# Spreading the k/v sums of batches 4 to 7 over four steps each, in a fused linear-attention and mixture-of-adapters kernel

## The chip, the cores and the metric

The kernel runs on one core of a Trainium2 chip. The metric is the device time of one execution in microseconds (us), lower is better. The core has a matrix engine (TensorE, "PE" in the profile, with its weight loads as "PEld"), a vector engine (DVE), an activation engine (ACT), a general engine (POOL) and an engine that here only issues transfers (SP). Each works through its own list of instructions in order; they wait for each other through semaphores. Matrix products land in PSUM, which has eight banks of 512 float32 columns on 128 partitions, and DVE or ACT must copy ("evacuate") them from there into SBUF before a bank can be written anew.

## The reference, cut to what matters

```
# q, k, v: (8 batches, 8 heads, 576 positions, 64)
phi(x)  = concat(relu(x) * cos(theta_pos), relu(x) * sin(theta_pos))   # 64 -> 128 features
kv      = sum over positions of phi(k)^T v          # one 128 x 64 matrix per batch and head
z       = sum over positions of phi(k)
attn    = phi(q) kv / (phi(q) . z + 1e-6)
x       = attn as 4608 rows of 512
logits  = x @ w_gate                                 # 8 experts
w       = softmax over the two largest logits, 0 for the other six
out     = x + sum over e of  w[e] * (x @ A[e]) @ B[e]   # A[e]: 512 x 16, B[e]: 16 x 512
```

The sums `kv` and `z` of a batch run over all its positions, so they must be complete before the first row of that batch can be computed.

## The kernel before, in words

The 4608 rows are cut into 36 token tiles of 128 rows. A pair of batches has nine of them; the middle one (n = 4, 13, 22, 31) holds the last positions of both batches. Each batch is read in nine position slices of 64 rows, s = 0 to 8.

One trip of the loop `for n in range(NT - 1)` is called step n here. The order of the work is written out by hand: each engine gets its instructions in the order in which the loop emits them. In a step, PE does in this order:

- `move_q(n + 1)` (its matmuls at L213, from tile 27 on at L201): multiplies q of the next tile by diagonal matrices, which transposes it and scales it. The result fills two tiles of the pool `qd`, which has two banks; ACT evacuates both with a relu (`evac_q`, L229).
- `logits` (L300) of the tiles that `early_at` names, 4 matmuls for each tile: gate logits and the A products, into the bank `za`.
- `kv` (L180) of the position slices that `kv_at` names for this step, 8 matmuls for each slice. All slices of a batch are accumulated in the two banks `cd0` and `cd1`; after a batch's ninth slice `kv_out` (L188, ACT) copies the sums to SBUF.
- the outputs of this step: `emit` calls `delta` (L366: x times the identity, L371: the B product) and `evac_o` (L397, ACT copy), then stores through SP. From step 28 on (`add=n > 27`) it calls `delta_add` instead, which leaves out the L366 matmul and lets POOL add x (L391).
- `transp_x` (L274), the transposition of this tile's x, which waits for DVE's `normalise` (L259, L266), and in one step of three `transp_z` (L348).
- `logits` of the tiles that `late_at` names, and `numden(n + 1)` (L247, L252), numerator and denominator of the next tile, which needs both evacuated q tiles.

An output needs one bank. While no k/v sum is open it takes `cd0` and `cd1` in turn (`own`). In a step that has an entry in `kv_at` it takes one from the pool `qd`, q's banks, in the profile `dx`. The pool hands its two banks out in turn: a request waits until the tile that had the bank two requests before has been evacuated.

`todo` is the list of token tiles whose gates are ready; three tiles are added in one step of three. A step takes one of them, or two if more than three are waiting.

`kv_at` is filled by `put(kv_at, step, (b, s))`. With `first` the first step that uses batch b, a batch's first four slices are in step `first - 2` and the other five in step `first - 1`. For batches 4 to 7 these are the steps 16 and 17, 20 and 21, 25 and 26, 29 and 30. The scaled k that the sums read (`kp`) is made by POOL, two instructions a slice (L156), in order of s, begun in step 12, 17, 20 and 23 for these batches after a relu by DVE (L165); slice 8 of batches 4 and 5 is made by ACT (L151). k, q and v are loaded by transfers that POOL issues some batches ahead.

Of the kernel before, what the change touches and what calls it, by code (L numbers as in the profile page):

```python
# [19 lines left out]
def kernel(ctx, tc, q, k, v, w_gate, A, Bw, out):  # L20
# [43 lines left out]
    def load_k(b, eng=None):  # L64
        load(eng or nc.gpsimd, k_b[b].rearrange("p g s d -> p g (s d)"), k, b)

    def load_q(b):
        load(nc.gpsimd, q_b[b].rearrange("p g s d -> p g (s d)"), q, b)

    def load_v(b):  # L70
        load(nc.gpsimd, v_b[b][:, 0:VN].rearrange("p (g x) -> p g x", g=G), v, b)
# [36 lines left out]
    def make_diag(s):  # L108
        for i, tab in enumerate((cos_tab, sin_tab)):
            nc.vector.tensor_scalar(out=diag[:, s, i], in0=ident, scalar1=tab[:, s:s + 1],  # L110
                                    scalar2=None, op0=ALU.mult)
# [6 lines left out]
    def load_weights():  # L118
        nc.gpsimd.dma_start(out=AW[:, 0:E].rearrange("p e c r -> p e (c r)"),
                            in_=A.rearrange("e (p c) r -> p e (c r)", c=DCH))  # L120
        nc.gpsimd.dma_start(out=AW[:, E, :, 0:E],
                            in_=w_gate.rearrange("(p c) e -> p c e", c=DCH))
        nc.gpsimd.dma_start(out=Ball, in_=Bw.rearrange("e r d -> (e r) d"))
# [35 lines left out]
    def scale_k(b, s, eng=("pool", "pool")):  # L159
        for i, e in enumerate(eng):  # L160
            scale_k1(b, s, i, e)
# [13 lines left out]
    def kv(b, s):  # L175
        first, last = kv_n[b] == 0, kv_n[b] == NS - 1
        kv_n[b] += 1
        for g in range(G):
            for par, pr in enumerate((lo, hi)):
                nc.tensor.matmul(out=kvz[par][:, g], lhsT=kp_t[b][pr, s, g],  # L180
                                 rhs=v_rhs(b, g, s, pr),
                                 start=(first and g == 0), stop=(last and g == G - 1))

    def kv_out(b):
        kv_t[b] = t = p_kv.tile([128, 2, G, W], BF16, name="kvsb")
        for par in range(2):
            src = kvz[par].rearrange("p g u d -> p g (u d)")[:, :, 0:W]
            nc.scalar.copy(t[:, par], src)  # L188
# [189 lines left out]
    def delta_add(n, own=True):  # L378

        if own:  # L380
            dx = cd[dx_n[0] % 2]
            dx_n[0] += 1
        else:
            dx = qd.tile([128, DM], FP32, name="dx", tag="qd")
        g = group_of[n]
        nc.tensor.matmul(out=dx, lhsT=zgT_t[g][:, n - groups[g][0], :], rhs=Ball,
                         start=True, stop=True)
        osb_t[n] = dx
        evac_o(n)
        t = osb_t[n]  # L390
        nc.gpsimd.tensor_tensor(out=t, in0=t, in1=xt_t.pop(n), op=ALU.add)  # L391
# [21 lines left out]
    kv_at, relu_at, pool_at, act_at, dve_at = {}, {}, {}, {}, {}  # L413

    def put(at, step, what):
        at.setdefault(step, []).append(what)
# [6 lines left out]
    for b in range(2, B):  # L423
        first = b // 2 * NS + b % 2 * 4
        at = {2: 5, 3: 8, 4: 12, 5: 17, 6: 20, 7: 23}[b]
        n_pool = {2: 5, 3: 7, 4: 8, 5: 8}.get(b, 9)
        for s0, s1 in ((0, 3), (3, n_pool)):
            put(relu_at, at, (b, s0, s1))
        for s in range(n_pool):
            put(pool_at, at, (b, s))  # L430
        for i in range(2):
            if n_pool <= 7:
                put(dve_at, at, (b, 7, i))
            if n_pool < 9:
                put(act_at, first - 4 + i, (b, 8, i))
            if n_pool == 5:
                put(act_at, first - 3 + i, (b, 6, i))
                put(act_at, first - 2, (b, 5, i))
        order = (7, 0, 1, 2, 3, 4, 8, 6, 5) if n_pool <= 7 else (0, 1, 2, 3, 4, 5, 8, 6, 7)
        if n_pool == 9:  # L440
            order = range(NS)
        for j, s in enumerate(order):
            put(kv_at, first - (2 if j < 4 else 1), (b, s))

# [17 lines left out]
    with tc.manual_schedule():  # L464
        for s in range(6):
            make_diag(s)
        wu = qd.tile([128, DM], FP32, name="wu", tag="qd")
        for i in range(24):
            nc.tensor.matmul(out=wu, lhsT=ones, rhs=wide, start=True, stop=True)  # L469
        for s in range(NS):  # L470
            scale_k(0, s, ("act" if s < 7 else "dve", "dve"))
            kv(0, s)
        nc.scalar.activation(warm, halfpi, AF.Sigmoid)
        for s in range(6, NS):
            make_diag(s)
        load_k(1)
        load_v(1)
        load_q(1)
        load_k(2)
        load_weights()  # L480
        load_v(2)
        load_q(2)
        load_k(3)
        load_v(3)
        load_k(4)
        load_q(3)
        load_v(4)
        kv_out(0)
        transp_q(0)
        evac_q(0, 0, "dve")  # L490
        evac_q(0, 1)
        numden(0)

        g10, g11, g12 = range(len(groups) - 3, len(groups))
        todo, held = [], []
        first_loads = persist.tile([1, 8], BF16, name="first_loads")

        def emit(d, own=True, eng="act", add=False):
            if add:
                delta_add(d, own)  # L500
            else:
                delta(d, own)
                evac_o(d, eng)
            if held is None:
                store(d)
            else:
                held.append(d)

        for n in range(NT - 1):
            if n > 0:  # L510
                g = move_at.get(n - 1, (None,))[0]
                evac_x(n - 1, g)
                if g is not None:
                    todo += groups[g]
            normalise(n)
            if n != 3:
                move_q(n + 1)
            for t in early_at.get(n, ()):
                logits(t)
            for b, s in kv_at.get(n, ()):  # L520
                kv(b, s)
                if kv_n[b] == NS:
                    kv_out(b)
            if n == 3:
                move_q(n + 1)
            for g in gate_a_at.get(n, ()):
                gate_a(g)
            for g in gate_b_at.get(n, ()):
                gate_b(g)
            now = todo[:2 if len(todo) > 3 else 1]  # L530
            del todo[:len(now)]
            for d in now:
                emit(d, n not in kv_at, add=n > 27)
            for g in gate_a_at.get(n, ()):
                gate_sig(g)
            transp_x(n)
            for g in move_at.get(n, ()):
                transp_z(g)
            for b, s, i in dve_at.get(n, ()):
                scale_k1(b, s, i, "dve")  # L540
            for b, s0, s1 in relu_at.get(n, ()):
                relu_k(b, s0, s1)
            for b, s in pool_at.get(n, ()):
                scale_k(b, s)
                if (b, s) == pool_at[n][-1]:
                    if b + 3 < B:
                        load_k(b + 3)
                    if b + 2 < B:
                        load_q(b + 2)
                    if b + 3 < B:  # L550
                        load_v(b + 3)
                    if b + 3 == B - 1:

                        nc.sync.dma_start(out=first_loads, in_=k_b[B - 1][0:1, 0, 0, 0:8])
                        for d in held:
                            store(d)
                        held = None
            for t in late_at.get(n, ()):
                logits(t)
            numden(n + 1)  # L560
            for b, s, i in act_at.get(n, ()):
                scale_k1(b, s, i, "act")


        evac_x(NT - 2)
        normalise(NT - 1)
        transp_z(g10)
        logits(NT - 2)
        evac_z(g10, [("act", 0, 3)])
        todo += groups[g10]  # L570
        for d in todo[:-3]:
            emit(d)
        transp_x(NT - 1)
        gate_a(g11)
        emit(todo[-3])
        gate_sig(g11)
        evac_x(NT - 1)
        logits(NT - 1)
        gate_b(g11)
        emit(todo[-2])  # L580
        gate_a(g12)
        transp_z(g11)
        evac_z(g11, [("act", 0, 2)])
        gate_sig(g12)
        emit(todo[-1])
        gate_b(g12)
        emit(NT - 3)
        transp_z(g12)
        evac_z(g12, [("dve", 0, 1)])
        emit(NT - 2)  # L590
        emit(NT - 1, eng="dve")
# [28 lines left out]
```

## Time and profile before

| | us |
|---|---|
| median of 3 runs | 116.12 (116.11 to 116.18) |
| the profiled execution, its own time | 116.03 |
| its span, first to last instruction | 114.3 |
| PE busy | 99.1 (87% of the span) |
| DVE busy | 79.8 (70%) |
| ACT busy | 77.6 (68%) |
| POOL busy | 71.2 (62%) |
| steps 14 to 30, from the first L213 of step 14 to the first L201 of step 31 | 45.77 (49.03 to 94.80) |

The profile is of one execution. Its page has the busy time of each engine, the span in 40 slices, the chain of work that ended last, and groups of instructions by line. A row of the timeline gives the start in us, the duration, the engine and line, the operands, the count of instructions merged into the row, and in brackets the idle time of the engine before it with what ended it. Matmuls overlap, and the ends of their records are modelled, so what a block of matmuls costs is read from its start to the start of the next block.

### The profile page before, as it was taken

The numbers are of one execution on the slowest core, as the hardware profiler recorded it, in microseconds if no ns is written. First come the engines' busy times: TensorE is split into PE (matmuls) and PEld (weight loads), VectorE is DVE, ScalarE is ACT, GpSimd is POOL, SyncE is SP. The second block draws the span as 40 slices with busy tenths as digits, with TensorE's granted clock in tenths as the row PEclk, the third lists the DMA queues.
The fourth block names the chain that finished last, engine by engine and source line by source line (L and its number), as shares of the span: only waits on it lengthen the run. The fifth ranks groups of instructions, "written<-read, shape, count | busy, mean of one in ns | idle before, by whom it ended". The sixth has DMA issues, their size and how long they took to land.

```text
span 114.3 us, 5021 instructions
## 1 busy us (share of the span) xinstructions
PE 99.1 (87%) x2101; PEld 73.9 (65%) x2101; DVE 79.8 (70%) x280; ACT 77.6 (68%) x169; POOL 71.2 (62%) x133
## 2 busy tenths in 40 slices
PE   3999677877998999999999999999998998978710
PEld 1347466756895688768787687787866886755200
DVE  5697588569849859697657966899459378796620
ACT  5087679846995847588758956777568668785720
POOL 5992222248986994999359989989940444744000
PEclk9999999999999999999999999999999999999996
DMA  3999999999999999999999999999989331433792
GB/s 43 384 207 209 212 202 207 205 187 210 207 212 205 207 209 209 209 207 208 207 209 207 207 208 231 279 336 379 356 324 383 126 100 71 154 127 141 269 331 88
DMA packets 19670, 24.77 MB, mean 217 GB/s; under 512 B 2624, under 2 KB 14528, under 8 KB 19648
## 3 DMA queue, kind: packets, MB, share of 16 engines
q0 software_dynamic: 13856, 13.84, 72.8%
q1 hardware_dynamic: 5792, 10.62, 26.4%
q8 instruction: 16, 0.26, 0.9%
q14 instruction: 6, 0.05, 0.1%
HBM read 28.85 MB, written 9.44 MB: 335 GB/s over the span
## 4 chain that ended last, share of the span: by engine, by line
PE 49%; DMA 26%; DVE 13%; issue 4%; POOL 3%; ACT 2%; POOLq 0%; ACTq 0%
DMA k<-in_k_dram 14%; DMA v<-in_v_dram 12%; PE cd L180 10%; PE za L300 8%; PE qd L213 6%; PE nd L252 6%; PE xz L274 5%; DVE xt L266 4%; PE qd L201 3%; PE dx L366 2%; DVE xT L280 2%; DVE zg L335 2%; PE cd L366 2%; PE cd L371 2%; PE xz L348 2%
## 5 line engine op out<-in xcount | busy, mean ns | idle before, releaser
L229 ACT ACTIVATE qpT<-qd 128x512 bf16<-128x512 f32 x71 | 38.6, 595 | 15.9 <-PE qd L213 11.7
L280 DVE COPY xT<-xz 128x512 bf16<-128x512 bf16 (+1 forms) x36 | 17.1, 475 | 15.2 <-PE xz L348 8.4
L156 POOL TENSOR_SCALAR kp<-k,cos_tab 128x256 bf16<-128x256 bf16 x46 | 22.5, 490 | 7.3 <-DVE k L165 6.4
L266 DVE TENSOR_TENSOR xt<-nd,rden 128x512 bf16<-128x512 f32 x36 | 24.9, 691 | 1.2
L156 POOL TENSOR_SCALAR kp<-k,sin_tab 128x256 bf16<-128x256 bf16 x46 | 21.8, 475 | 0.0
L180 PE MATMUL cd<-v,kp 64*128 64x128 bf16 x576 | 18.7, 217 | 0.7 <-DMA v<-in_v_dram 0.7
L274 PEld LDWEIGHTS <-xt 128*128 128x128 bf16 x144 | 10.4, 116 | 13.5 <-DVE xt L266 10.6
L252 PE MATMUL nd<-kvsb,qpT 128*128 128x65 bf16 (+1 forms) x320 | 17.2, 195 | 1.3 <-ACT qpT L229 0.5
L274 PE MATMUL xz<-ident,xt 128*128 128x128 bf16 x144 | 14.5, 223 | 4.3 <-DVE xt L266 4.2
L180 PEld LDWEIGHTS <-kp 64*128 64x128 bf16 x576 | 16.2, 94 | 2.5 <-issue 0.7
L213 PE MATMUL qd<-diag,q 128*64 128x128 bf16 x432 | 17.2, 222 | 0.1
L391 POOL TENSOR_TENSOR osb<-osb,xt 128x512 f32<-128x512 f32 x7 | 8.1, 1158 | 11.8 <-ACT osb L397 11.8
L397 ACT COPY osb<-cd 128x512 f32<-128x512 f32 x24 | 13.9, 594 | 1.3 <-PE cd L371 1.2
L252 PEld LDWEIGHTS <-qpT 128*128 128x128 bf16 (+1 forms) x320 | 12.5, 99 | 2.2 <-ACT qpT L229 1.2
L213 PEld LDWEIGHTS <-q 128*64 128x64 bf16 x432 | 12.9, 109 | 1.5 <-DMA q<-in_q_dram 0.3
L300 PE MATMUL za<-AW,xT 128*128 128x144 bf16 x140 | 12.2, 227 | 0.7 <-DVE zg L335 0.7
L247 PE MATMUL nd<-eps_hi,ones 128*128 128x4 bf16 x72 | 11.6, 169 | 0.0
L300 PEld LDWEIGHTS <-xT 128*128 128x128 bf16 x144 | 9.1, 98 | 2.9 <-DVE xT L280 0.8
L259 DVE RECIPROCAL rden<-nd 128x8 f32<-128x8 f32 x36 | 7.2, 201 | 5.2 <-PE nd L252 5.1
L62 POOL DMA_DIRECT2D v<-in_v_dram x8 | 6.2, 780 | 5.2 <-DMA q<-in_q_dram 4.3
L469 PE MATMUL wu<-wide,ones 128*128 128x512 bf16 x24 | 7.5, 488 | 2.0 <-DVE AW L115 2.0
L397 ACT COPY osb<-dx 128x512 f32<-128x512 f32 x11 | 6.4, 594 | 3.8 <-PE dx L371 3.0
(73 smaller groups left out, 137.7 us busy)
## 6 DMA issues: line engine op xcount, KB each, us to landing
out_dram<-osb SPq DMA_DIRECT2D x32, 256.0 KB, 3.7
v<-in_v_dram POOLq DMA_DIRECT2D x8, 576.0 KB, 17.9
q<-in_q_dram POOLq DMA_DIRECT2D x8, 576.0 KB, 16.2
k<-in_k_dram POOLq DMA_DIRECT2D x7, 576.0 KB, 15.5
k0f<-in_k_dram SPq DMA_DIRECT2D x1, 1152.0 KB, 5.4
out_dram<-osb SPq DMA_DIRECT2D x8, 128.0 KB, 3.8
AW<-in_moe_A_dram POOLq DMA_DIRECT2D x1, 128.0 KB, 18.2
Ball<-in_moe_B_dram POOLq DMA_DIRECT2D x1, 128.0 KB, 16.6
```

Of the source, the lines that this page charges most:

```text
L156: nc.gpsimd.tensor_scalar(out=dst, in0=src, scalar1=tab, scalar2=1.0, op0=ALU.mult, op1=ALU.mult)
L180: nc.tensor.matmul(out=kvz[par][:, g], lhsT=kp_t[b][pr, s, g], rhs=v_rhs(b, g, s, pr), start=(first and g == 0), stop=(last and g == G - 1))
L213: nc.tensor.matmul(out=t[cols, j, 2 * gi:2 * gi + 2, :], lhsT=q_b[b][:, 2 * gp + gi, s, :], rhs=diag[:, s, i], start=(j == 0 and gi == 0), ...
L229: nc.scalar.activation(t, src, AF.Relu)
L247: nc.tensor.matmul(out=nd[:, gg, D:4 * W:W], lhsT=ones, rhs=eps_hi, start=True, stop=False, skip_group_check=True)
L252: nc.tensor.matmul(out=nd[pr, gg, j * W:(j + 1) * W], lhsT=qpT[:, j, pr], rhs=kv_t[b][:, h % 2, h // 2, :], start=False, stop=(j == 3), sk ...
L266: nc.vector.tensor_tensor(out=x, in0=nd[:, :, :, 0:D], in1=rden.rearrange("p (g j) -> p g j", g=2).to_broadcast([128, 2, 4, D]), op=ALU.mult)
L274: nc.tensor.transpose(out=xz[:, c * 128:(c + 1) * 128], in_=x[:, c], identity=ident)
L280: nc.vector.tensor_copy(t[:, 0:c], xz[:, 0:c * 128].rearrange("p (c s) -> p c s", c=c))
L300: nc.tensor.matmul(out=za_t[g][:, i, :], lhsT=xT[:, c, :], rhs=AW[:, :, c, :], start=(c == 0 and i == 0), stop=(c == DCH - 1), skip_group_ ...
L391: nc.gpsimd.tensor_tensor(out=t, in0=t, in1=xt_t.pop(n), op=ALU.add)
L397: nc.scalar.copy(t, src)
```

## The change

For batches 4 to 7 the nine slices are spread over four steps: two slices each in the steps `first - 4`, `first - 3` and `first - 2`, three in `first - 1`. The second edit limits a step that has an entry in `kv_at` to one output. Batches 0 to 3 and the functions that are called stay as they are.

```
         for j, s in enumerate(order):
-            put(kv_at, first - (2 if j < 4 else 1), (b, s))
+
+            ahead = (2 if j < 4 else 1) if b < 4 else 4 - min(j // 2, 3)
+            put(kv_at, first - ahead, (b, s))
...
-            now = todo[:2 if len(todo) > 3 else 1]
+            now = todo[:2 if len(todo) > 3 and n not in kv_at else 1]
             del todo[:len(now)]
             for d in now:
                 emit(d, n not in kv_at, add=n > 27)
```

The steps with sums of batches 4 to 7 become 14 to 21 and 23 to 30, which are all steps from 14 to 30 but 22. In these the outputs go through `qd`.

## The prediction, written before the changed kernel had run

> **What bounds the kernel now.** I read the page first: busy times and the chain that ended last.
>
> ```profile
> PE 99.1 (87%) x2101; PEld 73.9 (65%) x2101; DVE 79.8 (70%) x280; ACT 77.6 (68%) x169; POOL 71.2 (62%) x133
> PE 49%; DMA 26%; DVE 13%; issue 4%; POOL 3%; ACT 2%; POOLq 0%; ACTq 0%
> ```
>
> PE is the busiest engine and has half of the chain; the loads' quarter of it is the start of the span, before the steps that change. So the next view was PE's timeline over two steps that hold the sums of batch 4 now, 16 and 17, read from start to start.
>
> ```profile
> 53.96 0.64 PE L213 MATMUL qd<-diag,q 128*64 128x128 bf16 x16
> 54.53 1.07 PE L180 MATMUL cd<-v,kp 64*128 64x128 bf16 x32
> 55.53 0.39 PE L366 MATMUL dx<-xt,ident 128*128 128x512 bf16 x1
> ...
> 56.41 0.39 PE L274 MATMUL xz<-ident,xt 128*128 128x128 bf16 x4
> 56.63 0.17 PE L247 MATMUL nd<-eps_hi,ones 128*128 128x4 bf16 x1
> ...
> 57.02 0.69 PE L213 MATMUL qd<-diag,q 128*64 128x128 bf16 x16
> 57.65 0.67 PE L300 MATMUL za<-AW,xT 128*128 128x144 bf16 x8
> 58.25 1.29 PE L180 MATMUL cd<-v,kp 64*128 64x128 bf16 x40
> 59.47 0.39 PE L366 MATMUL dx<-xt,ident 128*128 128x512 bf16 x1
> ```
>
> Nothing waits here: one block follows the other. It gives the price list. The transposition of q is 0.57 (53.96 to 54.53). A block of 32 sum matmuls is 1.00, one of 40 is 1.22: 0.0275 for a matmul and a fixed 0.12 for a block. Two outputs are 0.88 (55.53 to 56.41), so one is 0.44 and its B product alone about 0.22. x is 0.22, numerator and denominator 0.39. Last, the steps where PE does wait. Each row of the view of stretches is a step: start and end, its length, then busy time and number of instructions of PE, PEld, DVE, ACT and POOL, the granted clock, DMA share and GB/s. They are the steps 14, 16, 19, 22, 24, 27, 28, 31 and 33.
>
> ```profile
> 49.03:51.92 2.89, 2.71 (x45) 1.99 (x42) 2.23 (x6) 2.52 (x7) 2.89 (x7) 1.00 1.21 207
> 53.96:57.02 3.06, 3.06 (x70) 2.35 (x68) 2.08 (x6) 2.45 (x7) 1.29 (x2) 1.00 1.21 207
> 63.00:65.03 2.03, 1.92 (x35) 1.23 (x32) 1.96 (x6) 2.03 (x6) 2.03 (x6) 1.00 1.22 209
> 71.86:73.72 1.86, 1.82 (x42) 1.18 (x38) 1.60 (x6) 1.44 (x4) 1.86 (x5) 1.00 1.14 277
> 76.01:78.12 2.11, 2.11 (x39) 1.42 (x37) 2.04 (x11) 1.60 (x5) 2.11 (x5) 1.00 1.08 373
> 84.40:86.37 1.97, 1.97 (x55) 1.35 (x52) 1.90 (x10) 1.39 (x4) 0.00 (x0) 1.00 0.90 338
> 86.37:88.58 2.21, 1.64 (x51) 1.12 (x49) 2.04 (x6) 1.66 (x5) 0.00 (x0) 1.00 1.04 378
> 94.80:96.84 2.04, 1.70 (x53) 1.18 (x49) 1.86 (x5) 1.56 (x5) 1.17 (x1) 1.00 0.03 8
> 98.76:100.72 1.96, 1.73 (x55) 1.23 (x52) 1.89 (x10) 1.60 (x4) 1.16 (x1) 1.00 0.39 142
> ```
>
> A step without sums whose contents by the price list are q 0.57, one output 0.44, x 0.22 and nd 0.39 should take 1.62. Step 19 takes 2.03, so PE waits 0.41 in it; step 22 waits 0.24; step 24, with 4 logit matmuls at 0.26 more, 0.23. In these ACT and DVE are busy 1.4 to 2.0: they set the short steps, PE the long ones. That is where the change can win: it moves PE work from the long steps into the short ones.
>
> **The change part by part.** (a) More blocks. Eight steps get a block of 16 sum matmuls: 14, 15, 18, 19, 23, 24, 27, 28. The number of matmuls stays, so a batch goes from 2 to 4 fixed parts: 8 x 0.12 = 0.96. Where logits come right before the sums there is more:
>
> ```profile
> 74.29 0.67 PE L300 MATMUL za<-AW,xT 128*128 128x144 bf16 x8
> ...
> 74.80 0.38 PE L366 MATMUL cd<-xt,ident 128*128 128x512 bf16 x1
> ```
>
> Eight logit matmuls take 0.51 ahead of an output but 0.60 ahead of sums (57.65 to 58.25). Sums run in another tile shape (64\*128) than logits and outputs (128\*128), so I take 0.10 for each change of shape after logits. That meets five of the new steps (15, 18, 23, 24, 27): 0.50. Together +1.46 of PE. No block of 16 is in this trace; the ends are 0.44 (16 x 0.0275, no fixed part) and 0.66 (both changes paid), and I take 0.56, or 0.66 after logits, by the line through 32 and 40, which are the nearest rows. The ends move the sum by -1.46 and +0.30.
>
> The Trainium skill, "TensorEngine Tiling (Array Packing)", Key Properties, states that changing the tiling mode, not just the tile, drains TensorE; it speaks against spreading the sums, and the 0.10 and 0.12 above agree with it. The drain of about 128 cycles that the skill's "TensorE: Matmul & The Clock Gate" (Step-by-step) gives would be an estimated 0.053 at 2.4 GHz, and with two for each of eight blocks 0.85 in place of 1.46, so a time 0.6 lower; the rows decide.
>
> (b) Outputs. Following `todo` through both rules: steps 14 to 30 emit 20 outputs now (5 to 24) and 18 after (5 to 22). The double steps 14, 16 and 18 become single, 22 becomes double, and the missing two are caught up as second outputs of 31 and 33. Three of the outputs are cheap `delta_add` ones, now (tiles 22 to 24) as after (20 to 22). So two full outputs leave the stretch: -0.88. In 31 and 33 they are B products alone, 0.22 each, and those steps have contents of about 1.2 and 1.5 in 2.04 and 1.96: the waits cover them (without that cover +0.44). ACT copies and POOL adds one more tile in each of the two, where ACT is busy 1.6 of 2.0 and POOL 1.2: a small delay is possible, none is counted. From step 33 on the list of outputs is that of now, so the tail, the stores on SP's queue included, stays.
>
> (c) Waits of PE that the added 0.56 covers. 19: 0.41. 24: 0.23. 22: 0.24, by its second output. 27: contents 1.69 (q's transposition is 0.38 here, by the next fence) in 1.97; of the 0.28 about 0.11 is the wait of (d), so 0.17. 14:
>
> ```profile
> 51.04 0.66 PE L300 MATMUL za<-AW,xT 128*128 128x144 bf16 x8 [0.18 <-DVE zg L335]
> ...
> 86.37 0.45 PE L201 MATMUL qd<-diag,q 64*64 64x64 bf16 x32
> 86.75 0.39 PE L386 MATMUL cd<-Ball,xT 128*128 128x512 bf16 x1
> 87.53 0.41 PE L274 MATMUL xz<-ident,xt 128*128 128x128 bf16 x4 [0.39 <-DVE xt L266]
> ...
> 88.34 0.30 PE L252 MATMUL nd<-kvsb,qpT 128*128 128x65 bf16 x4 [0.18 <-ACT qpT L229]
> ```
>
> In 14 the logits start 2.01 after the step because DVE's gate must end first. Sums 0.56 and one output instead of two put PE there at 1.79, so 0.2 of 0.34 stays: 0.14 won. Step 28 has contents of 1.21 (0.38 + 0.22 + 0.22 + 0.39) in 2.21: 1.00 of waits. Of these 0.38 stays by (d), 0.62 is won. Sum (c): -1.81.
>
> (d) New waits, the price of q's banks. In each step with sums the output takes a `qd` bank, so it waits for ACT's first evacuation of q, and everything on PE behind it (x, nd, the next q) waits too; and the next transposition of q waits for ACT's copy of the output.
>
> Rows of ACT's timeline, then of PE's:
>
> ```profile
> 54.48 1.08 ACT L229 ACTIVATE qpT<-qd 128x512 bf16<-128x512 f32 x2
> 80.33 0.59 ACT L397 COPY osb<-dx 128x512 f32<-128x512 f32 x1 [0.61 <-PE dx L371]
> 87.20 1.09 ACT L229 ACTIVATE qpT<-qd 128x512 bf16<-128x512 f32 x2 [0.55 <-PE cd L386]
> 80.74 0.67 PE L201 MATMUL qd<-diag,q 64*64 64x64 bf16 x32
> 81.34 0.67 PE L300 MATMUL za<-AW,xT 128*128 128x144 bf16 x8
> ```
>
> In step 16 ACT starts 0.52 after PE's transposition; one evacuation is about 0.6, and PE follows ACT after 0.05 (87.20 + 1.09, then 88.34). So the bank is free at 1.17. With 32 sums PE comes at 1.57, with 16 at 1.13: a wait of 0.04, in 16, 19 and 25; with logits ahead of the sums PE comes at 1.4 or later. From step 26 on the transposition fills both banks at once, so it waits for the output's copy at its very start: step 26 after the dx of 25 takes 0.60 (80.74 to 81.34; the copy ends at 80.92) against 0.38 undisturbed. That 0.22 comes newly in 28 and 29. In 28 ACT can start only when both tiles are done, so the output waits about 0.18 as well; these are the 0.38 of (c). New on top: 3 x 0.04 + 0.2 = +0.3. Ends: 0 for each of the 12 steps with 16 sums, and 0.31, the lateness of ACT in step 28 now (87.20 is 0.83 after 86.37, against 0.52), so 0 to +3.7; I stand near the low end because the rows of step 16, which is of the same kind, give 0.04.
>
> (e) Earlier need of data.
>
> ```profile
> 60.00 0.47 POOL L156 TENSOR_SCALAR kp<-k,sin_tab 128x256 bf16<-128x256 bf16 x1
> 26.01 0.76 POOL L62 DMA_DIRECT2D v<-in_v_dram  x1
> DMA to landing us min/median/max: 7.6/17.9/21.1
> ```
>
> POOL's list is not changed. Batch 5 is the closest: its slices 0 and 1 are scaled by 60.5 (the sine of slice 1 is the row of 60.00), counted from a relu early in step 17, which starts at 57.02. Slice 0 is needed 0.57 + 0.36 into step 18, thus 61.6 on the old clock and about 61.1 with the shortened steps 16 and 17; slice 1 a quarter of a microsecond later. It holds by some tenths. v of batch 4 is issued at 26.01 and lands by 47.1 even at the slowest landing; it is needed at 49.6. Cost 0; should POOL be late, up to 0.5 once.
>
> Sum: 1.46 - 0.88 - 1.81 + 0.32 = -0.9. On the profiled execution's own 116.03 (span 114.3) that is 115.1; the median of the runs, 116.12, is 0.09 above it, so 115.2.
>
> **Rivals.** First, q's banks bind (slower). Place: L366 in the 12 steps with 16 sums, behind ACT's first evacuation. (a) to (c) give -1.23; the wait decides from 0.10 in each of the 12 steps on. At 0.2 it is +2.4 - 1.2 = +1.2: 117.3. For it: the margin in step 16 is nil, ACT is late by 0.3 in step 28 now, and after the change each late copy delays the next transposition, which delays ACT. Against it: steps 17, 21 and 26 follow outputs in q's banks now and wait 0 to 0.22 (17: 0.06, 57.02 to 57.65), and a step has only about 1.7 of regular ACT work.
>
> The Trainium skill has the same fear in "TensorEngine Tiling (Array Packing)", PSUM Bottleneck: a faster TensorE leaves the PSUM copies as the bottleneck.
>
> Second, no change: the short steps are set by the loop nd, DVE, x, nd rather than by PE, and work put into them does not shorten the long ones as much as counted. If a third of (c) is won, 0.6 instead of 1.81, the sum is +0.3 and with fewer switches about 0: 116.1. For it: DVE is busy 2.04 of 2.11 in step 24 and 1.90 of 1.97 in step 27. Against: in the long steps PE has no wait, and they get shorter by 0.4 to 0.9 each.
>
> Third, scaled k comes late (slower): POOL holds up steps 18 to 21 and then everything behind; 0.5 for each of batches 5 and 6 makes 116.2 or more. The margins of (e) speak against it. That the outputs don't go through `qd` cannot be: `n not in kv_at` decides it.
>
> **How the numbers follow.** Forecast and near it (114.6 to 115.8) 0.58; the banks 0.25; no change 0.12; late k 0.05. A difference of 0.2% (0.23 us) is about what can be told from none. So faster 0.58, same 0.12, slower 0.30. The range goes from 114.6 (no new wait and 0.2 less for the blocks) to 117.0, with the outer part of the banks' case, about 0.15, above it and 0.05 below; the forecast's own range is 114.6 to 115.8.
>
> **What the profile after should show.** L180 in blocks of 16 and 24 that take 0.56 and 0.78; steps 16, 17, 20, 21, 25, 26, 29 and 30 shorter by 0.3 to 0.9, 15, 23, 24 and 27 longer by 0.4 to 0.7; little idle PE ahead of L366; the first L201 of step 31 near 94.0. I am wrong if L366 waits for ACT by more than 0.1 in most steps, if L201 waits by more than 0.3, or if steps 18 to 21 wait for POOL.

## The result, and the profile after

The changed kernel takes 115.44 us (115.39 to 115.54, 4 runs) against 116.12 (116.06 to 116.18, 4 runs) on the same chip: a ratio of 0.9939, 95% interval 0.9921 to 0.9956. It is faster by 0.6%. The profiled execution took 115.39 with a span of 113.6; before, 116.03 and 114.3. From the page of the changed kernel, the busy times and the chain by engine:

```profile
PE 99.4 (88%) x2099; PEld 74.2 (65%) x2099; DVE 80.9 (71%) x280; ACT 78.1 (69%) x169; POOL 73.2 (64%) x135
PE 52%; DMA 26%; DVE 11%; POOL 3%; issue 2%; ACT 2%; POOLq 0%; DVEq 0%; ACTq 0%
```

PE is still the bound, and its share of the chain is larger. Next, the view of stretches for the same nine steps as in the prediction (14, 16, 19, 22, 24, 27, 28, 31, 33), then the whole of steps 14 to 30, with the same columns:

```profile
49.06:51.95 2.89, 2.86 (x59) 2.27 (x56) 2.31 (x6) 2.23 (x6) 2.89 (x7) 1.00 1.21 208
54.65:56.86 2.21, 2.21 (x53) 1.73 (x50) 2.08 (x6) 2.02 (x6) 0.60 (x1) 1.00 1.21 207
62.56:64.83 2.27, 2.23 (x51) 1.78 (x48) 1.88 (x6) 2.08 (x6) 2.27 (x7) 1.00 1.21 208
70.76:72.79 2.03, 2.03 (x42) 1.43 (x38) 1.75 (x6) 1.61 (x5) 2.03 (x5) 1.00 1.18 237
75.74:78.39 2.65, 2.61 (x56) 1.95 (x54) 2.22 (x11) 1.52 (x4) 2.65 (x6) 1.00 1.06 390
83.80:86.26 2.46, 2.46 (x71) 1.87 (x69) 2.03 (x10) 1.52 (x4) 0.09 (x1) 1.00 0.84 313
86.26:88.49 2.23, 2.04 (x66) 1.65 (x64) 1.88 (x6) 1.75 (x5) 0.00 (x0) 1.00 0.72 265
94.02:96.06 2.04, 1.91 (x54) 1.20 (x48) 1.86 (x5) 1.56 (x5) 1.16 (x1) 1.00 0.22 79
98.02:99.97 1.95, 1.95 (x57) 1.32 (x54) 1.88 (x10) 1.57 (x4) 1.71 (x2) 1.00 0.41 154
...
49.06:94.02 44.96, 44.65 (x1020) 35.06 (x1017) 34.01 (x106) 33.02 (x72) 33.26 (x67) 1.00 1.00 239
```

Step 16 went from 3.06 to 2.21. Steps 24 and 27 grew, from 2.11 to 2.65 and from 1.97 to 2.46, because they hold sums now. Steps 14, 31 and 33 kept their length with more PE work in them. The stretch shrank from 45.77 to 44.96, by 0.81, and the rest of the execution gave 0.17 of that back. PE's timeline shows steps 16 and 17, and then 28, of the changed kernel:

```profile
54.65 0.64 PE L213 MATMUL qd<-diag,q 128*64 128x128 bf16 x16
55.22 0.62 PE L180 MATMUL cd<-v,kp 64*128 64x128 bf16 x16
55.82 0.38 PE L366 MATMUL dx<-xt,ident 128*128 128x512 bf16 x1
...
57.43 0.67 PE L300 MATMUL za<-AW,xT 128*128 128x144 bf16 x8
58.04 0.84 PE L180 MATMUL cd<-v,kp 64*128 64x128 bf16 x24
58.81 0.39 PE L366 MATMUL dx<-xt,ident 128*128 128x512 bf16 x1
...
86.84 0.62 PE L180 MATMUL cd<-v,kp 64*128 64x128 bf16 x16
87.65 0.38 PE L386 MATMUL dx<-Ball,xT 128*128 128x512 bf16 x1 [0.19 <-ACT qpT L229]
```

A block of 16 sums is 0.60 in step 16 with the small wait of the output in it, a block of 24 is 0.77, and only in step 28 does the profile mark the output as waiting for ACT's evacuation of q.

### The profile page after: what moved, and what is told of

It reads as the page before. It is cut to its first block, busy times and chain, and to the rows that moved or that the text cites. A ratio compares the mean times of both kernels' runs of the same rounds, so it can differ in the third digit from the quotient of the medians.

```text
span 113.6 us, 5022 instructions
## 1 busy us (share of the span) xinstructions
PE 99.4 (88%) x2099; PEld 74.2 (65%) x2099; DVE 80.9 (71%) x280; ACT 78.1 (69%) x169; POOL 73.2 (64%) x135
## 4 chain that ended last, share of the span: by engine, by line
PE 52%; DMA 26%; DVE 11%; POOL 3%; issue 2%; ACT 2%; POOLq 0%; DVEq 0%; ACTq 0%
DMA k<-in_k_dram 14%; DMA v<-in_v_dram 12%; PE cd L180 10%; PE za L300 8%; PE qd L213 7%; PE nd L252 6%; PE xz L274 5%; PE dx L366 4%; DVE xt L266 4%; PE qd L201 3%; PE dx L371 3%; PE xz L348 2%; DVE zg L335 2%; DVE xT L280 2%; ACT qpT L229 1%
## 5 line engine op out<-in xcount | busy, mean ns | idle before, releaser
L180 PE MATMUL cd<-v,kp 64*128 64x128 bf16 x576 | 20.1, 217 | 0.8 <-DMA v<-in_v_dram 0.8
L180 PEld LDWEIGHTS <-kp 64*128 64x128 bf16 x576 | 16.2, 94 | 3.4 <-issue 0.8
L252 PE MATMUL nd<-kvsb,qpT 128*128 128x65 bf16 (+1 forms) x320 | 16.9, 194 | 1.0 <-DVE qpT L231 0.5
L391 POOL TENSOR_TENSOR osb<-osb,xt 128x512 f32<-128x512 f32 x9 | 10.2, 1160 | 9.5 <-ACT osb L397 9.0
L397 ACT COPY osb<-dx 128x512 f32<-128x512 f32 x18 | 10.6, 591 | 5.3 <-PE dx L371 5.0
L252 PEld LDWEIGHTS <-qpT 128*128 128x128 bf16 (+1 forms) x320 | 12.4, 99 | 1.7 <-ACT qpT L229 0.7
L247 PE MATMUL nd<-eps_hi,ones 128*128 128x4 bf16 x72 | 11.6, 169 | 0.0
L397 ACT COPY osb<-cd 128x512 f32<-128x512 f32 x17 | 9.7, 599 | 1.3 <-PE cd L371 1.3
```

The costliest lines, as they stand in the source:

```text
L247: nc.tensor.matmul(out=nd[:, gg, D:4 * W:W], lhsT=ones, rhs=eps_hi, start=True, stop=False, skip_group_check=True)
L252: nc.tensor.matmul(out=nd[pr, gg, j * W:(j + 1) * W], lhsT=qpT[:, j, pr], rhs=kv_t[b][:, h % 2, h // 2, :], start=False, stop=(j == 3), sk ...
L397: nc.scalar.copy(t, src)
```

## The experiments

All ratios are to the kernel before, run beside it on the same chip. Lengths of steps 14 to 30 come from PE's timeline, from the first transposition of q of step 14 to that of step 31. Four kernels were profiled twice; for three of them the two lengths agree within 0.01, the fourth is told of at the end. A whole execution can shift by some tenths in the first 45 us (step 14 starts between 48.90 and 49.71 in the profiles of kernels that are alike up to there), so these lengths are the sharper measure.

**Each edit alone.** First the spreading without the limit (the changed kernel with one line undone), then the limit without the spreading (that line alone in the kernel before):

```
-            now = todo[:2 if len(todo) > 3 and n not in kv_at else 1]
+            now = todo[:2 if len(todo) > 3 else 1]
```

> Only the first edit: the sums of batches 4 to 7 over four steps, while a step may still emit two outputs. Theory A (the gain is PE work put into waits, minus shape changes, and the two outputs that leave steps 14 to 30 are needed for it): 1.46 for the blocks, nothing for outputs, waits covered in 14, 19, 24, 27 and 28 of about 1.8, new waits 0.3, so 0.0 against before: 116.1. Theory B (spreading the sums is the gain, the limit to one output does nothing): 115.4, as the changed kernel.

> Only the second edit: sums in two steps as before, but one output at most in a step with sums. The second output of step 16 (0.44 of PE, no wait there) moves to step 24, where 0.23 of it falls into a wait. Theory A: 0.2 faster than before, 115.9. Theory B: no change, 116.1. If the limit alone makes the gain: 115.4.

Spreading alone took 116.57, ratio 1.0035 (1.0018 to 1.0051): slower. The limit alone took 115.86, ratio 0.9969 (0.9956 to 0.9982), a stretch of 45.56, the 0.2 less of theory A (0.36 by the medians, on a chip where the kernel before scattered from 115.84 to 116.68). It holds back only the second output of step 16, because in the kernel before only eight of these steps have sums. Theory B falls, and so does the thought that the limit alone makes the gain. Rows of the view of stretches for the run that only spreads: steps 14 to 30, and step 28.

```profile
49.71:95.94 46.23, 44.92 (x1012) 35.41 (x1021) 33.26 (x106) 34.00 (x74) 33.26 (x67) 1.00 1.00 241
87.90:90.41 2.51, 2.04 (x67) 1.66 (x64) 1.88 (x6) 1.75 (x5) 0.00 (x0) 1.00 0.74 272
```

The stretch is 0.46 longer than before where theory A had 0.0. Step 28 explains 0.28 of the miss: it takes 2.51 here and 2.23 in the changed kernel, with the same contents, because ACT starts to evacuate q 0.3 later. The trace names no cause for that lateness; the kernel before shows the same in its step 28, as the prediction noted. The last section has which kernels show it.

**Only the outputs deferred.** If the limit gains and the spreading loses, the gain may be in when outputs are made. This run leaves the sums of the kernel before where they were and gives each step the number of outputs that it has in the changed kernel:

```
-            now = todo[:2 if len(todo) > 3 else 1]
+            now = todo[:2 if len(todo) > 3 and not (13 < n < 31 and n != 22) else 1]
```

> The kernel before with the sums where they were (two steps a batch), but with one output at most in steps 14 to 30 except 22: the same output in every step as in the changed kernel, so that two outputs go to steps 31 and 33. Theory A (of the changed kernel's gain the deferred outputs are most, spread sums and their shape changes about cancel): 16 loses 0.44, 18 about 0.42, 14 nothing since its logits wait for DVE's gate, 22 gains 0.17, so 0.5 to 0.7 faster than before: 115.5. Theory B (outputs can only be deferred at a gain when the sums are spread): as the run with the limit in steps with sums alone, 115.9, or slower.

It took 115.27, ratio 0.9927 (0.9914 to 0.9940): at least as fast as the changed kernel, with no sum moved. Theory A holds. Its rows: steps 14 to 30, then 16, 18, 19, 22 and 28.

```profile
49.16:93.90 44.74, 43.25 (x1011) 34.39 (x1019) 33.07 (x106) 32.39 (x72) 33.27 (x67) 1.00 1.01 243
54.10:56.72 2.62, 2.57 (x66) 2.15 (x64) 2.07 (x6) 2.01 (x6) 1.25 (x2) 1.00 1.21 207
60.35:62.32 1.97, 1.97 (x40) 1.42 (x37) 1.90 (x10) 1.48 (x5) 1.97 (x5) 1.00 1.22 208
62.32:64.20 1.88, 1.72 (x34) 1.23 (x32) 1.81 (x6) 1.88 (x6) 1.88 (x5) 1.00 1.21 207
71.02:73.05 2.03, 2.03 (x42) 1.43 (x38) 1.75 (x6) 1.61 (x5) 2.03 (x6) 1.00 1.14 282
85.75:87.68 1.93, 1.54 (x52) 1.09 (x49) 1.86 (x6) 1.66 (x5) 0.00 (x0) 1.00 1.04 384
```

The stretch is 1.03 shorter than before, 0.22 shorter than that of the changed kernel. Step 16 loses its second output (3.06 to 2.62), 18 too (2.30 to 1.97). Step 19 takes 1.88 where it took 2.03, with nothing moved into or out of it: a part of its wait was ACT, which without the second output copy of step 18 begins to evacuate q 0.52 after the start of the step instead of 0.65. Step 28 takes 1.93 instead of 2.21, as ACT is not late in it.

**The price of a change of tile shape.** In the changed kernel the logits of a step (128\*128 tiles) come before its sums (64\*128) and the output (128\*128) after. One run puts the sums first, one splits them around the logits:

```
-            for t in early_at.get(n, ()):
-                logits(t)
             for b, s in kv_at.get(n, ()):
                 kv(b, s)
                 if kv_n[b] == NS:
                     kv_out(b)
+            for t in early_at.get(n, ()):
+                logits(t)
```

```
-            for t in early_at.get(n, ()):
-                logits(t)
-            for b, s in kv_at.get(n, ()):
+            sums = kv_at.get(n, ())
+            cut = 1 if n > 13 and early_at.get(n) else 0
+            for b, s in sums[:cut]:
+                kv(b, s)
+            for t in early_at.get(n, ()):
+                logits(t)
+            for b, s in sums[cut:]:
                 kv(b, s)
```

> The changed kernel with the sums ahead of the early logits in each step, so that logits and output, of one tile shape, follow each other. Nothing is left out or added. If a change of the tile shape of the matmuls costs 0.10 on PE, one change goes in 11 steps (15, 17, 18, 20, 21, 23, 24, 26, 27, 29, 30): 1.1 less than the changed kernel, 114.3. If the 0.10 before sums is not the shape but a wait of the sums for something else, or if the steps are set by ACT and DVE: no difference, 115.4. Scaled k is needed 0.26 to 0.6 earlier, in batch 5 some tenths may come back as waits for POOL.

> The changed kernel with the sums of a step cut in two around its early logits, in the same 11 steps: one slice ahead of the logits, the rest behind. The same matmuls, one more block of sums in each of the 11 steps. By the fixed part of 0.12 of a block: 11 x 0.12 = 1.3 more than the changed kernel, 116.7. If blocks have no fixed part and only the matmuls count: 115.4.

Sums first took 114.06, ratio 0.9813 (0.9792 to 0.9834); split took 116.35, ratio 1.0012 (0.9997 to 1.0026). From PE's timeline, step 17 with sums first:

```profile
56.59 0.64 PE L213 MATMUL qd<-diag,q 128*64 128x128 bf16 x16
57.17 0.84 PE L180 MATMUL cd<-v,kp 64*128 64x128 bf16 x24
57.94 0.67 PE L300 MATMUL za<-AW,xT 128*128 128x144 bf16 x8
58.45 0.38 PE L366 MATMUL dx<-xt,ident 128*128 128x512 bf16 x1
```

and step 15 with the sums split:

```profile
52.97 0.40 PE L180 MATMUL cd<-v,kp 64*128 64x128 bf16 x8
53.30 0.42 PE L300 MATMUL za<-AW,xT 128*128 128x144 bf16 x4
53.66 0.40 PE L180 MATMUL cd<-v,kp 64*128 64x128 bf16 x8
53.98 0.39 PE L366 MATMUL dx<-xt,ident 128*128 128x512 bf16 x1
```

Eight logit matmuls take 0.51 ahead of an output (57.94 to 58.45) and took 0.61 ahead of sums (57.43 to 58.04 above). Step 17 takes 3.07 instead of 3.17, and all steps with logits and sums but 24, 27, 29 and 30 shrink by the same 0.10 or 0.11. Split, step 15 takes 2.80 instead of 2.70, and eight of the eleven steps grow by 0.10 or 0.11; 27 and 30 grow by 0.05 and 0.04, and 24 not at all. So one change of shape is 0.10 on PE. The price rests on these steps. The totals of steps 14 to 30, 0.93 shorter with sums first and 0.95 longer with the sums split, look like eleven times 0.10, but the first is so in part by accident: in that profile step 29 is 0.37 longer, while 24, 28 and 30 are 0.15 to 0.22 shorter. A second profile of the same kernel, the second of the four corners below, is 1.31 shorter than the changed kernel beside it.

The split adds one block of sums to a step, and with it one change of shape, for the same 0.10. So a block has no fixed part besides its changes of shape. Blocks of 16, 24, 32 and 40 sums take 0.55, 0.77, 1.00 and 1.22, which is 0.028 for a matmul and 0.10 fixed; the 0.12 that was expected was a little high.

No run changes the shape alone: the sums also differ from the logits in their operands. That it is the shape is supported by `numden`, whose L252 comes in two shapes behind the same L247. Rows of the changed kernel, from the steps 16 and 21:

```profile
56.47 0.17 PE L247 MATMUL nd<-eps_hi,ones 128*128 128x4 bf16 x1
56.50 0.28 PE L252 MATMUL nd<-kvsb,qpT 128*128 128x65 bf16 x4
...
70.16 0.17 PE L247 MATMUL nd<-eps_hi,ones 128*128 128x4 bf16 x1
70.26 0.32 PE L252 MATMUL nd<-kvsb,qpT 128*64 128x65 bf16 x8
```

In the same shape L252 starts 0.03 behind L247, in another shape 0.10.

**The cover of q's banks.** The output put ahead of the sums:

```
-            for b, s in kv_at.get(n, ()):
...
+            if n < 14:
+                for b, s in kv_at.get(n, ()):
...
             for d in now:
                 emit(d, n not in kv_at, add=n > 27)
+            if n > 13:
+                for b, s in kv_at.get(n, ()):
+                    kv(b, s)
+                    if kv_n[b] == NS:
+                        kv_out(b)
```

> The changed kernel with the output of a step ahead of the sums instead of behind them, from step 14 on. The same instructions. If the sums hide the wait of the output for ACT's first evacuation of q, PE now comes to the output 0.57 (no logits), 0.83 (four) or 1.08 (eight logit matmuls) after the start of the step and waits until 1.17: 0.6 in 16, 19, 25, 28, half of that in 14, 0.34 in six steps, 0.09 in five, together 5 to 6, and the last sums of a batch come later for the copy that nd needs: 120.5 to 122. If the output does not wait for q's banks: 115.4.

It took 122.06, ratio 1.0524 (1.0509 to 1.0539). Step 16 of this run on PE, then the output and the sums of step 17:

```profile
55.58 0.64 PE L213 MATMUL qd<-diag,q 128*64 128x128 bf16 x16
56.74 0.38 PE L366 MATMUL dx<-xt,ident 128*128 128x512 bf16 x1 [0.53 <-ACT qpT L229]
57.28 0.62 PE L180 MATMUL cd<-v,kp 64*128 64x128 bf16 x16 [0.17 <-issue]
...
59.64 0.38 PE L366 MATMUL dx<-xt,ident 128*128 128x512 bf16 x1
60.17 0.85 PE L180 MATMUL cd<-v,kp 64*128 64x128 bf16 x24 [0.15 <-issue]
```

The output starts 1.16 after the step: the bank is free at 1.17, as worked out from the evacuation. The wait is real, and 16 sum matmuls are just about enough to hide it. From the output to the sums it is 0.54 (56.74 to 57.28) where an output alone is 0.44. The 0.10 is the price of a change of shape, and not of the wait: step 17 has it too (59.64 to 60.17), where the output did not wait. (The brackets show more, as they count from the modelled end of the matmul before.) In the five steps without early logits (14, 16, 19, 25 and 28) this order has one change of shape more than the changed kernel, an estimated 0.5 in all, which the expected 5 to 6 left out. With it the sum is 5.5 to 6.5, and the loss is 6.6. The granted clock was 0.94 in the profiled execution, which took 122.34, but 0.99 to 1.00 in the other three, which took 122.04 to 122.07, so the clock is not behind the loss.

**What spreading is worth.** The deferred outputs with sums first, in two steps; then all four corners (sums in four or two steps, logits or sums first, the outputs the same in all four), run side by side on one chip:

```
-            now = todo[:2 if len(todo) > 3 else 1]
+            now = todo[:2 if len(todo) > 3 and not (13 < n < 31 and n != 22) else 1]
...
-            for t in early_at.get(n, ()):
-                logits(t)
             for b, s in kv_at.get(n, ()):
...
+            for t in early_at.get(n, ()):
+                logits(t)
```

> As the run that only defers outputs, with the sums ahead of the early logits: 6 of its steps with sums have early logits (17, 20, 21, 26, 29, 30), so 6 x 0.10 less than that run: 114.9. The difference to the changed kernel with sums first (114.06) is what spreading is worth once a block of sums pays one shape change less: 0.8. If spreading is worth nothing even then: 114.1.

> The four corners on one chip, all with the same output in every step: sums over four steps or over two, logits or sums first. This is the changed kernel itself. Against the kernel before: 0.6% faster, as measured.

> Four steps, sums first. If 11 shape changes at 0.10 are all that the order is worth, 0.95% less than the first corner: a ratio of 0.984 to before. If the 0.3 that PE waited without a visible cause in step 29 of its profile is the profiled execution's alone, 0.3 less in the others: 0.981.

> Two steps, logits first: only the outputs are deferred. If spreading is worth nothing by itself: the ratio of the first corner within 0.2%, 0.993. If spreading has a part in the gain: above 0.996.

> Two steps, sums first: six shape changes less than the third corner, 0.5% less, 0.988. Its distance to the second corner is what spreading is worth when sums come first: 0.3 us by the lengths of steps 14 to 30 in the profiles (44.03 against 44.33), 0.6 to 0.8 by the medians of the two earlier sessions.

The first of these took 114.69, ratio 0.9886 (0.9872 to 0.9899): 0.58 less than the run that only defers outputs, against the six times 0.10 that were expected. The corners:

| | logits first | sums first |
|---|---|---|
| four steps | 115.46, 0.9947 (0.9934 to 0.9960) | 114.38, 0.9866 (0.9834 to 0.9897) |
| two steps | 115.24, 0.9925 (0.9913 to 0.9937) | 114.66, 0.9877 (0.9864 to 0.9890) |

The stretch of steps 14 to 30 of the four, from left to right and top to bottom, each row from its own kernel's view of stretches:

```profile
49.06:94.01 44.95, 44.08 (x1009) 35.08 (x1017) 34.04 (x106) 33.01 (x72) 33.25 (x67) 1.00 1.00 239
49.18:92.82 43.64, 42.69 (x1009) 35.05 (x1017) 34.08 (x106) 32.86 (x72) 33.27 (x67) 1.00 1.02 244
49.10:93.83 44.73, 43.25 (x1012) 34.40 (x1019) 33.08 (x106) 32.38 (x72) 33.27 (x67) 1.00 1.02 244
49.02:93.36 44.34, 42.54 (x1010) 34.45 (x1017) 33.40 (x106) 32.95 (x72) 33.32 (x68) 1.00 1.03 245
```

With logits first, spreading costs 0.22 in the stretch and 0.2% in the times (intervals that barely overlap). The third and the fourth corner came out as was worked out for a spreading that is worth nothing by itself with logits first (0.993 and 0.988). The order of logits and sums is worth 1.08 us with four steps (115.46 against 114.38), the eleven times 0.10 that were expected; of the two values named for the second corner, 0.984 lies within its interval and 0.981 outside.

With sums first spreading saves 0.70 in the stretch of these profiles, of the 0.8 that was worked out, and 0.30 in the first pair of profiles (44.33 against 44.03, where step 29 holds the gap told of at the end). In the times of the four corners only 0.28 us shows, within the interval of the four-step kernel, whose runs scatter from 113.95 to 115.30. The 114.06 of the same kernel above lies lower. How much of the 0.70 arrives at the end of the execution stays open, between 0.3 and 0.7.

**A version that beats both.** Sums first, and batch 3 spread over three steps as well:

```
-            ahead = (2 if j < 4 else 1) if b < 4 else 4 - min(j // 2, 3)
+            ahead = (2 if j < 4 else 1) if b < 3 else 3 - j // 3 if b == 3 else 4 - min(j // 2, 3)
```

> The changed kernel with sums first, and batch 3 over three steps (10, 11, 12 with three slices each) instead of 11 and 12. Step 11 loses 8 sum matmuls (0.22), step 12 loses 16 (0.44), step 10, where the logits wait for DVE's gate, gets 24 (0.77) of which about 0.15 is not covered: 0.5 less than with sums first, 113.55. If v or scaled k of batch 3 is late in step 10: no gain or slower than 114.06.

It took 113.59, ratio 0.9799 (0.9780 to 0.9818), the lowest time of all, though the interval overlaps that of sums first on the other chip (0.9792 to 0.9834). From its timeline, steps 10, 11 and 12 take 3.15, 2.57 and 3.37 (before 2.98, 2.79 and 3.82): +0.17, -0.22 and -0.45, as worked out; v and scaled k of batch 3 are in time.

## Why the prediction was right, step by step

The forecast was 115.2, a gain of 0.9; measured is 115.44, a gain of 0.7. In the stretch where the sum was made, the gain is 0.81. That it fits so well is in part luck: the outputs gave more than was counted (1.03 against 0.88), and the moved sums cost 0.22 where their terms came to about nothing. Of the signs that were named, the blocks, the first L201 of step 31 (94.02) and the steps that grow (by 0.49 to 0.66) came as said; of those that shrink, 29 won only 0.24.

(a) held, and its price was the one disputed: 16 sums take 0.55 after logits (0.56 forecast), 24 take 0.77 (0.78), and the two runs that add or take away a change of shape in 11 steps both give 0.10 each. The fixed part of a block and the price of a change after logits are the same thing: the eight new blocks bring 13 more changes of shape (one in each of 14, 19 and 28, two in each of the five with logits), so an estimated 1.3 in place of 1.46. The rule from the Trainium skill's page "TensorEngine Tiling (Array Packing)" (Key Properties, a change of tiling mode drains TensorE) agrees with that 0.10. The estimate of 0.053, which the prediction worked out from the drain in the Trainium skill's page "TensorE: Matmul & The Clock Gate" (Step-by-step), was too low: the runs show 0.10.

(b) held and is the whole of the gain, but not only as PE work. Two outputs fewer in steps 14 to 30 were put at -0.88; the run that only defers them shows -1.03 in the stretch. Step 16 gives 0.44 of it and step 18 0.33, step 14 nothing, as its logits wait for DVE's gate, and 22 takes 0.17 back: that makes 0.60. Most of the rest is waits for ACT that go away, 0.28 in step 28 and 0.15 in step 19. The waits of steps 31 and 33 took the two in: 2.04 and 1.95 after, 2.04 and 1.96 before.

(c) is the step that was weakest. The waits were there and the sums were put into them, but I counted some of them as free room that belonged to the second outputs: without those, step 19 takes 1.88 rather than 2.03, and step 28's 1.00 included 0.28 in which ACT was late. In step 24 a wait grew instead: DVE's relu of batch 7 took longer, and the logits, which need the evacuation of x behind it, started 0.68 after the step instead of 0.63 before and 0.57 without a wait. Rows of DVE's, POOL's and PE's timelines of the changed kernel:

```profile
73.79 2.05 DVE L165 TENSOR_SCALAR k<-k 128x768 bf16<-128x768 bf16 x2
75.76 0.61 DVE L280 COPY xT<-xz 128x896 bf16<-128x896 bf16 x1
...
74.68 0.48 POOL L156 TENSOR_SCALAR kp<-k,sin_tab 128x256 bf16<-128x256 bf16 x1
75.65 0.53 POOL L156 TENSOR_SCALAR kp<-k,cos_tab 128x256 bf16<-128x256 bf16 x1 [0.49 <-PE xz L348]
...
76.42 0.42 PE L300 MATMUL za<-AW,xT 128*128 128x144 bf16 x4
```

In the kernel before the two relus took 1.29 together. The first of them ends when POOL pauses: at 75.38 here, 0.22 after the run of scalings that ends at 75.16, and at 75.59 before, 0.21 after 75.38. That distance is 0.21 or 0.22 in all 13 profiles in which POOL was scaling when the relu began, and the relu takes 0.82 to 1.73 in them; in the run with the output first POOL had just stopped, and it takes 0.35. So the changed kernel, in which DVE comes to the relu earlier, waits longer in it, and it is POOL's list that sets the start of the logits in step 24. Why DVE has to wait for POOL the profiles do not show.

By the prediction's own terms (a), (c) and (d) came to about zero (1.46 - 1.81 + 0.32); measured, with outputs held the same, they are +0.22. So the opening claim, that the change wins by moving PE work from long steps into short ones, was wrong as the main cause: with logits first, what the sums win in the waits is paid back in changes of shape.

(d) held: the output waits 0.04 in step 16 by the lengths (0.60 against 0.55 or 0.56 without a wait), 0.25 in 28 (0.81 from the sums to the output; 0.18 forecast). The first rival, that q's banks bind, needed 0.10 in each of 12 steps; no step but 19 (0.66 for its block) and 28 reached it. The transposition of q takes 0.58 and 0.59 in steps 28 and 29 against 0.38, close to the 0.22 that was counted. The run with the output first shows what keeps the rival away: without the sums as cover the kernel takes 6.6 us more, most of it this wait. The second rival, no change, has this much truth that, with logits first, the spreading by itself is worth nothing. The third, late k, did not happen: no wait for POOL stands ahead of L180 in the changed kernel.

(e) held, and the tail did not: the sum had it unchanged, and what follows step 30 is longer now. Step 32 is 0.04 longer, and from the start of step 34 to the end of PE's last output it is 8.47 instead of 8.34. This comes with the deferred outputs and not with the sums: it is 8.34 to 8.36 in the three kernels that emit the outputs as before (the limit alone and the spreading alone among them) and 8.47 to 8.53 in all that defer them. ACT and POOL have two more outputs there (POOL 7.93 busy from step 31 on against 5.79), which was named as a possible small delay and not counted. The rows of what follows step 30, of the changed kernel:

```profile
94.02:109.17 15.15, 12.54 (x247) 7.49 (x241) 11.17 (x40) 11.75 (x27) 7.93 (x7) 1.00 0.59 198
```

and of the kernel before:

```profile
94.80:109.79 14.99, 12.08 (x244) 7.35 (x239) 11.16 (x40) 10.96 (x25) 5.79 (x5) 1.00 0.45 155
```

That POOL is the cause was not tested.

## What to carry to other kernels

When one change moves two things, write the sum so that each has its own term, and run each alone: here the deferred outputs carried the whole gain, and the moved sums that gave the change its name cost 0.2 us by themselves. The second edit did not do it alone either: it holds outputs back only in steps with sums, and on its own it was worth 0.2 in the stretch. On a saturated TensorE, order the blocks of a step so that those of one tile shape stand together: swapping two loops saved more here (1.08 us with four steps) than the change itself (0.62 on the same chip). A wait that a profile shows is not yet room to fill; ask first what made it, because it may go away with the work that you move elsewhere.

## What was not expected

ACT began an evacuation 0.3 late in step 28 in the three kernels that emit their outputs as before or nearly so (before, limit alone, spreading alone: 0.83, 0.85 and 1.02 after the start of the step) and not in their counterparts that defer them (0.55 in the run that only defers, 0.74 in the changed kernel, where spread sums make it later). So it goes with the time at which outputs are made, and the 0.28 of step 28 is a steady part of the gain; what makes ACT late the profiles do not show. In the first profile with sums first PE waited 0.31 in the middle of the logits of step 29, for nothing that the profile shows:

```profile
89.19 0.30 PE L300 MATMUL za<-AW,xT 128*128 128x144 bf16 x2 [0.31 <-issue]
```

In the second profile of the same kernel, the second corner, that step took 2.65 instead of 3.13, which is why the two lengths of its stretch differ, 44.03 and 43.64. Such an event is worth half of what was measured here, so a comparison of two profiles needs the lengths of the other steps beside it. That DVE's relus of batch 7 took 1.29 before and 2.05 after with the same operands, because they end with POOL's scalings, was not foreseen either.
